# A fused Nyström-attention and Fourier-MLP kernel: Pool takes a share of VectorE's work at the start, and the inverse's iterations carry B instead of C·v

## The chip, the cores and the metric

The kernel runs on one core of one Trainium2 chip. The metric is the device time of one execution in microseconds (us). The engines that matter are TensorE (PE in the profile, with PEld for its weight loads), VectorE (DVE), ScalarE (ACT), GpSimd (POOL) and SyncE (SP), which issues all DMAs. The kernel before takes 1015.25 us, the median of three runs (1013.77 to 1017.46).

## The reference

Eight batches, eight heads, 576 tokens, head size 64. The first half is attention by 32 landmarks, with an iterated inverse; the second half is a real 2-D Fourier transform, a layer norm and an MLP from 512 to 2048 and back. The weights come as float64, the rest as float32.

```python
def sm(a, b):                        # softmax of scale * a @ b.T
    ...
q_lm, k_lm = means of q and k over 18 tokens (32 landmarks)
A, Bm, C = sm(q, k_lm), sm(q_lm, k_lm), sm(q_lm, k)
Z = Bm.T / (norm1(Bm) * norminf(Bm) + 1e-6)
for _ in range(6):
    Z = 2 * Z - Z @ Bm @ Z
x = A @ Z @ C @ v                    # heads joined: (8, 576, 512)
u = x + real(fft(fft(x, axis=1), axis=2))
un = (u - mean(u)) / sqrt(var(u) + 1e-6)
out = u + relu(un @ w_ch1) @ w_ch2
```

## The kernel before, in words

**Two halves on one TensorE.** Every float32 matrix that needs its precision is split into a high and a low float16 half (`split`, line 245: ACT writes the high half, DVE the rest by one SCALAR_TENSOR_TENSOR) and multiplied in three float16 matmuls (`mm3`). The MLP is the bulk: tokens go in chunks of 256 (`TCH` = 2 tiles of 128), and each chunk multiplies with sixteen pieces of w1 (output `h` in PSUM, 256 columns) and sixteen pieces of w2 (accumulators `acc`, 512 columns). `mlp` (line 879) runs the chunks, with the w2 products two steps behind the w1 products.

**Attention, per batch.** `tokens` (line 410) takes the landmark sums, the scales, splits q (two halves `e` of the heads, line 459), makes the softmax A (three blocks `u`, lines 468 to 495), A's transposed halves, and A's folds over mirrored tokens (F1, F2, Fh, lines 518 to 528), whose product with cosine and sine tables is `CS`. `landmarks` (line 552) makes the softmaxes B and C, sets up the inverse (E and RE, lines 637 to 643), transposes C's exponentials, multiplies them by v (lines 669 to 679), runs six iterations on the pair RE (lines 683 to 696), and then forms the landmark weights Wx and Wt and their table product WC. RE has 96 columns for each of two groups of heads: 32 hold the power of the residual matrix, 64 hold C·v, which the iterations multiply by the inverse as they go. A block-diagonal B (`Bbd`) comes in at the end. `mix` (line 743) puts A, WC, Wx and CS together into the rows `u`, and `norm` (line 816) normalises them and hands them to the MLP as `unT`, the transposed halves. For the first two batches transposes go over TensorE, later ones over DMA transposes.

**Weights.** `weights` (line 265) decodes each float64 piece of 128x512 as it lands: ACT makes its magnitude (`prepare`, four pieces ahead, `PREP`), a low part comes from DVE (even pieces: a shift, line 332) or ACT (odd pieces: a byte conversion, line 335), and DVE joins the two (line 336). Pieces feed a Gram matrix on TensorE (`squares`), from which a scale comes (`scale`, after 18 decoded pieces for w1, after all 32 for w2). `halve` (line 312) then splits a piece by that scale.

**What sets the order.** The order of TensorE's work is written out by a planner: the generators above are threads with priorities (attention, weights, MLP, line 948 on), `now` is a model of TensorE's time, `Timed` (line 114) models the other engines by a fixed and a per-element cost, and `till` (line 224) makes a thread wait until its inputs should be ready, and, with `banks`, until that many PSUM banks should be free. While a thread waits, others put matmuls into the queue; while all wait and the accumulator bank is not yet in use, filler matmuls on `idle` are issued. TensorE then executes that order as it stands, waiting wherever the model was too early. The instructions of the other engines are ordered by the framework, and `Timed` adds order constraints that keep VectorE and ScalarE from waiting for late inputs.

Of the kernel before, what the change touches and what calls it, by code (L numbers as in the profile page):

```python
# [18 lines left out]
P = 128  # L19
# [94 lines left out]
class Timed:  # L114
# [6 lines left out]
    def __getattr__(self, name):  # L121
        call = getattr(self.engine, name)

        def emit(out, *args, **kw):
# [5 lines left out]
            start = max([self.kernel.now] + [self.kernel.there.get(a.name, 0.0) for a in aps])  # L130
            end = max(self.free, start + self.fixed + rate * n + 0.1)
            self.kernel.there[out.name] = end
            for a in aps[1:]:
                self.kernel.read[a.name] = end
# [4 lines left out]
            late = max([late] + [self.kernel.there.get(a.name, 0.0) for a in aps if a.name in self.kernel.slow and a is not out])  # L139
            if self.engine is self.kernel.nc.gpsimd:  # L140
                self.kernel.slow.add(out.name)
            else:
                self.kernel.slow.discard(out.name)
# [10 lines left out]
class Kernel:  # L154
    def __init__(self, ctx, tc, NB, q, k, v, w1, w2, t1, t1t, t2, diag, mask, out):
# [7 lines left out]
        self.loads = {}  # L163
# [12 lines left out]
        self.whole = [self.cp.tile([P, 512 * NF + OFF], F32, name=f"w{w}") for w in range(2)]  # L176
        self.mask = const(mask, [P, 6], F32, "mask")
# [26 lines left out]
        self.arrival(1.7)  # L204

# [59 lines left out]
    def weights(self):  # L265
# [12 lines left out]
        def prepare(i):  # L278
# [6 lines left out]
            mags.append(mag)  # L285

# [9 lines left out]
        def scale(w):  # L296
# [4 lines left out]
            yield self.till(a2)  # L301
# [10 lines left out]
        def halve():  # L312
            w, f = pieces[sum(self.split_w)]
            self.split(hl[w][f][:, 0], hl[w][f][:, 1], slots[w][f], sc[:, w : w + 1])
            self.split_w[w] = f + 1

        for i, (w, f) in enumerate(pieces):
# [10 lines left out]
            low = self.wraw[i].rearrange("p (m x) -> p m x", x=2)[:, :, 0]  # L328
            x, dst = mags[i].bitcast(I32), slots[w][f].bitcast(I32)
            (A if i % 2 else V).late = self.raw_there[i]  # L330
            if i % 2 == 0:
                V.tensor_scalar(dst, low, 29, None, ALU.logical_shift_right)
            else:
                byte = self.wraw[i].bitcast(mybir.dt.uint8).rearrange("p (m x) -> p m x", x=8)[:, :, 3]
                A.activation(dst, byte, AF.Copy, scale=2.0**-5, bias=-0.484375)
# [6 lines left out]
            yield max(0.0, max(self.V.free, self.G.free) - self.now - WT)  # L342
            if i == NF + 1:
                yield from scale(0)
            for _ in range(PACE if es else 0):
                if self.split_w[0] < NF:
                    halve()
                    yield max(0.0, max(self.V.free, self.G.free) - self.now - WT)
# [61 lines left out]
    def tokens(self, b, st):  # L410
# [33 lines left out]
        yield self.till(kb, more=AM) + (HOLD if b == 1 else 0.0)  # L444
# [14 lines left out]
        for e in range(2):  # L459
            qs = loads[e][1][:, 0:NQ].rearrange("p (x t) -> p x t", t=2 * SEG)  # L460
            for t, a, w in ((qm[e], 1, 128), (qr[e], 129, 16)):
                split(*(t[:, y].rearrange("p r (s t) -> p (r s) t", t=w) for y in range(2)), qs[:, :, a : a + w], rq)
# [5 lines left out]
        for u in range(3):  # L468
            yield self.till(*qhs)
# [24 lines left out]
            (self.G if b > 0 else V).tensor_tensor(av, av, bc(asum), ALU.mult)  # L494
# [24 lines left out]
        for x, op in enumerate((ALU.add, ALU.subtract)):  # L519
            V.tensor_tensor(F1[x], aes[0], aes[1], op)  # L520
        for x, op in enumerate((ALU.add, ALU.subtract)):
            F2 = self.mid()[:, 0:512]
            for k in range(2):
                (V if x == 0 else G).tensor_tensor(F2[:, 256 * k : 256 * k + 256], F1[k][:, 0:256], F1[k][:, 256:512], op)
# [4 lines left out]
        Fs.append(hl)  # L529
        CS = self.big().bitcast(F16).rearrange("p (g y x t) -> p g y x t", g=2, y=2, x=2)  # L530
# [20 lines left out]

    def landmarks(self, b, st):
# [7 lines left out]
        RE = sm.tile([P, 2, 96], F32, name="RE", bufs=3)  # L560
# [60 lines left out]
        yield self.till(nrm)  # L621
# [12 lines left out]
        Bbd = sm.tile([P, 2, 4, 32], F32, name="Bbd", bufs=1)  # L634
        V.tensor_tensor(Bbd, wide(nrm[:, :, 0, :], 32), m4g(32), ALU.mult)
        yield self.till(BTd, Ces[0])
# [7 lines left out]
        ETs = []  # L644
        for g in range(2):
            if b < 2:
# [405 lines left out]
```

## Time and profile before

| | |
|---|---|
| median of three runs | 1015.25 us |
| the profiled execution | 1017.3 us |
| its span, first to last instruction | 1015.5 us |
| busy: PE, DVE, ACT, POOL | 961.4, 595.1, 332.1, 125.8 us |
| filler matmuls on `idle` | 22.0 us |

In the profile L137 is the line of the helper through which DVE, ACT and POOL instructions go, and L233 that of the matmul helper, so groups are told apart by the names of the tiles. The tile `w` holds both weights, `at` is a working PSUM bank, `big`, `mid` and `row` are working buffers. A busy share of PE counts the filler too. In a timeline each row has its start, its length (several like instructions in a row merged, with their count), the engine, and in brackets how long the engine sat idle before it and what ended that.

### The profile page before, as it was taken

The page shows a single profiled execution, that of the slowest core. Times are in us where ns is not written, and L with a number is a line of the kernel's source. Part 1 is how long each engine was busy: PE and PEld are TensorE (multiplying, and loading weights), DVE is VectorE, ACT ScalarE, POOL GpSimd, SP SyncE. Part 2 cuts the span into 40 slices and gives each one's busy share as a digit, 9 for nine tenths or more (in the row PEclk, how much of TensorE's full clock was granted, in tenths as well). Part 3 has the DMA queues.
Part 4 walks back from the last instruction along what each step waited for, and adds up shares of the span by engine and source line. Part 5 has one row for each costly group of instructions (what it writes and reads, how often), then busy time and mean ns, then how long its engine had stood idle before and what let it go on. Part 6 is the DMA issues. An engine that isn't in the chain of part 4 may idle for free.

```text
span 1015.5 us, 20853 instructions
## 1 busy us (share of the span) xinstructions
PE 961.4 (95%) x8701; PEld 667.2 (66%) x8701; DVE 595.1 (59%) x1599; ACT 332.1 (33%) x708; POOL 125.8 (12%) x144
## 2 busy tenths in 40 slices
PE   6769889899999999999999999999999999999998
PEld 4658556567665777666666677666666676666665
DVE  7889776886367636386267736784463834351111
ACT  5668643243134213153134213332322322111110
POOL 0000000014011400123001400231020310110000
PEclk8979999899999999999999999999999999999999
DMA  9854104133302430134202240225020200120000
GB/s 329 284 207 154 53 1 167 22 66 83 122 6 62 93 121 2 42 58 108 84 24 41 51 167 1 63 48 180 1 54 21 49 13 22 21 53 21 1 21 21
DMA packets 97774, 74.66 MB, mean 74 GB/s; under 512 B 68112, under 2 KB 86544, under 8 KB 97552
## 3 DMA queue, kind: packets, MB, share of 16 engines
q1 hardware_dynamic: 97680, 73.34, 24.7%
q8 instruction: 68, 1.11, 0.5%
q14 instruction: 26, 0.21, 0.1%
HBM read 48.02 MB, written 9.44 MB: 57 GB/s over the span
## 4 chain that ended last, share of the span: by engine, by line
PE 45%; issue 23%; DVE 6%; POOL 3%; DMA 2%; ACT 1%; SPq 0%; POOLq 0%; DVEq 0%; ACTq 0%
PE h L233 20%; PE acc L233 20%; PE at L233 6%; POOL mid L137 1%; DVE mid L137 1%; POOL row L137 1%; DMA mid<-mid 1%; DVE big L137 1%; DVE h L137 1%; DVE asum L137 1%; DVE row L137 1%; DVE u L137 1%; DMA unT<-row 0%; SPq L661 0%; DMA out_dram<-u 0%
## 5 line engine op out<-in xcount | busy, mean ns | idle before, releaser
L233 PE MATMUL h<-unT,w 128*128 128x256 f16 x3456 | 411.9, 273 | 3.9 <-DMA unT<-row 2.5
L233 PEld LDWEIGHTS <-w 128*128 128x128 f16 (+1 forms) x3584 | 345.7, 98 | 77.9 <-issue 7.9
L233 PE MATMUL acc<-w,h 128*128 128x512 f16 x1632 | 386.1, 382 | 2.4 <-DVE w L137 2.4
L233 PEld LDWEIGHTS <-h 128*128 128x128 f16 x1632 | 157.9, 99 | 167.8 <-issue 14.5
L137 DVE SCALAR_TENSOR_TENSOR h<-h 128x512 f16<-128x512 f32 x136 | 93.4, 687 | 196.6 <-ACT h L137 196.1
L137 ACT ACTIVATE h<-h 128x512 f16<-128x512 f32 x136 | 80.9, 595 | 300.8 <-PE h L233 288.4
L137 POOL TENSOR_TENSOR r<-ve,mhalf 128x2 f32<-128x2 f32 (+1 forms) x20 | 13.7, 684 | 475.9 <-DVE ve L137 471.3
L137 POOL TENSOR_TENSOR mid<-mid 128x640 f16<-128x640 f32 (+2 forms) x36 | 40.4, 1144 | 99.7 <-ACT mid L137 82.7
L137 DVE TENSOR_TENSOR mid<-mid 128x256 f32<-128x256 f32 (+3 forms) x52 | 39.6, 796 | 12.5 <-POOL mid L137 6.4
L137 DVE TENSOR_REDUCE lm<-big 128x32 f32<-128x576 f32 (+1 forms) x48 | 44.2, 939 | 3.3 <-DMA big<-k_dram 3.1
L233 PEld LDWEIGHTS <-big 128*128 128x128 f16 (+1 forms) x864 | 40.2, 103 | 8.2 <-issue 2.1
L137 DVE SCALAR_TENSOR_TENSOR u<-at,scw,row 128x128 f32<-128x128 f32 (+3 forms) x120 | 38.7, 389 | 9.7 <-DMA out_dram<-u 6.9
L137 ACT CAST row<-row 128x512 f16<-128x512 f32 (+1 forms) x40 | 20.7, 551 | 72.0 <-DVE row L137 72.0
L233 PEld LDWEIGHTS <-mid 64*128 64x128 f16 (+1 forms) x624 | 30.2, 96 | 20.4 <-issue 13.9
L137 POOL TENSOR_TENSOR row<-row 128x512 f16<-128x512 f32 (+1 forms) x33 | 35.5, 1091 | 32.9 <-ACT row L137 32.9
L137 DVE SCALAR_TENSOR_TENSOR row<-at,scw,row 128x262 f32<-128x262 f32 (+1 forms) x48 | 21.4, 486 | 29.9 <-ACT row L137 20.2
L233 PE MATMUL at<-RE,E 128*128 128x96 f32 (+1 forms) x192 | 30.8, 279 | 8.6 <-DVE RE L137 8.6
L233 PEld LDWEIGHTS at<-RE,E 128*128 128x128 f32 x192 | 27.1, 192 | 16.1 <-DVE RE L137 9.4
L137 DVE SCALAR_TENSOR_TENSOR u<-acc,wsc,u 128x512 f32<-128x512 f32 x36 | 26.7, 748 | 11.1 <-PE acc L233 10.9
L137 DVE TENSOR_TENSOR E<-at,mask 128x256 f32<-128x256 f32 x40 | 16.6, 416 | 28.0 <-PE at L233 28.0
L233 PE MATMUL at<-mid,big 128*128 128x262 f16 (+1 forms) x288 | 32.7, 282 | 0.1
L137 DVE SCALAR_TENSOR_TENSOR big<-big,aq_r 128x1024 f16<-128x1024 f32 (+1 forms) x32 | 25.8, 840 | 3.5 <-ACT big L137 3.5
(174 smaller groups left out, 911.0 us busy)
## 6 DMA issues: line engine op xcount, KB each, us to landing
w<-w_dram SPq DMA_DIRECT2D x22, 512.0 KB, 7.0
big<-v_dram SPq DMA_DIRECT2D x16, 640.0 KB, 9.4
big<-q_dram SPq DMA_DIRECT2D x16, 584.0 KB, 5.6
big<-k_dram SPq DMA_DIRECT2D x16, 576.0 KB, 4.6
out_dram<-u SPq DMA_DIRECT2D x36, 256.0 KB, 2.0
big<-w_dram SPq DMA_DIRECT2D x10, 512.0 KB, 4.7
t<-t_dram SPq DMA_DIRECT2D x1, 1048.0 KB, 10.3
unT<-row SPq DMA_TRANSPOSE x64, 2.4
```

Of the source, the lines that this page charges most:

```text
L137: ins = call(out, *args, **kw)
L233: self.nc.tensor.matmul(out, a, b, start=start, stop=stop, skip_group_check=True)
```

## The change

Pool (`self.G`) takes these from VectorE: the low part of the even weight pieces, now a byte conversion, issued in `prepare`; the two elementwise steps of every third piece's halving (high half still by ScalarE); for batches 0 and 1 the scaling and low half of q for e = 1, the differences of F2 and the low half of the second Fh; for batch 0 the scaling of A's softmax and the difference of F1.

The inverse's iterations carry B (32 columns) in place of C·v (64 columns); the result is made block-diagonal (`Yd`) and multiplied by `R0`, the scaled C·v, at the end. C's transposes and its product with v move into a thread of their own, `values`, which runs beside the iterations. Pool's instructions are held in the order in which the program issues them. Seven waits of the planner now also count a free PSUM bank (`banks=1`), the weights' pace no longer counts Pool's time, times are kept per offset for tiles that are one allocation, and for batches after 0 two buffers of `mix` lie in memory that the raw weights no longer need.

```diff
@@ Timed.emit
-            start = max([self.kernel.now] + [self.kernel.there.get(a.name, 0.0) for a in aps])
+            key = self.kernel.key
+            start = max([self.kernel.now] + [self.kernel.there.get(key(a), 0.0) for a in aps])
...
             if self.engine is self.kernel.nc.gpsimd:
-                self.kernel.slow.add(out.name)
+                self.kernel.slow.add(key(out))
+                if self.log:
+                    info = mybir.DependencyInfo(mybir.DependencyClass.NoSync, mybir.DependencyReason.DATA)
+                    self.kernel.tc.add_manual_dep(ins.ins, self.log[-1][1], info, reason="order")
+                self.log.append((start, ins.ins.name))
@@ weights, prepare
+            E = (self.G, A)[i % 2]
+            byte = self.wraw[i].bitcast(mybir.dt.uint8).rearrange("p (m x) -> p m x", x=8)[:, :, 3]
+            if i % 2 == 0:
+                E.tensor_scalar(dst, byte, 2.0**-5, -0.484375, ALU.mult, ALU.add)
+            else:
+                E.activation(dst, byte, AF.Copy, scale=2.0**-5, bias=-0.484375)
@@ weights, halve
-            self.split(hl[w][f][:, 0], hl[w][f][:, 1], slots[w][f], sc[:, w : w + 1])
+            if f % 3 == 2:
+                self.G.tensor_scalar(slots[w][f], slots[w][f], sc[:, w : w + 1], None, ALU.mult)
+                A.copy(hl[w][f][:, 0], slots[w][f])
+                self.G.tensor_tensor(hl[w][f][:, 1], slots[w][f], hl[w][f][:, 0], ALU.subtract)
+            else:
+                self.split(hl[w][f][:, 0], hl[w][f][:, 1], slots[w][f], sc[:, w : w + 1])
@@ weights, the loop over pieces
-            if i % 2 == 0:
-                V.tensor_scalar(dst, low, 29, None, ALU.logical_shift_right)
-            else:
-                ...
-            yield max(0.0, max(self.V.free, self.G.free) - self.now - WT)
+            yield max(0.0, self.V.free - self.now - WT)
@@ tokens
-        yield self.till(kb, more=AM) + (HOLD if b == 1 else 0.0)
+        yield self.till(kb, banks=1, more=AM) + (HOLD if b == 1 else 0.0)
...
+            if b < 2 and e == 1:
+                self.G.tensor_scalar(loads[e][1][:, 0:NQ], loads[e][1][:, 0:NQ], rq, None, ALU.mult)
...
+                if b < 2 and e == 1:
+                    A.copy(hi, qs[:, :, a : a + w])
+                    self.G.tensor_tensor(lo, qs[:, :, a : a + w], hi, ALU.subtract)
...
-            (self.G if b > 0 else V).tensor_tensor(av, av, bc(asum), ALU.mult)
+            self.G.tensor_tensor(av, av, bc(asum), ALU.mult)
...
-            V.tensor_tensor(F1[x], aes[0], aes[1], op)
+            (V if b > 0 or x == 0 else self.G).tensor_tensor(F1[x], aes[0], aes[1], op)
...
-                (V if x == 0 else G).tensor_tensor(F2[...], F1[k][:, 0:256], F1[k][:, 256:512], op)
+                (V if x == 0 else self.G).tensor_tensor(F2[...], F1[k][:, 0:256], F1[k][:, 256:512], op)
...
-            G.tensor_tensor(Fh[:, 1], F2, Fh[:, 0], ALU.subtract)
+            (V if b < 2 and x == 0 else self.G).tensor_tensor(Fh[:, 1], F2, Fh[:, 0], ALU.subtract)
@@ landmarks (C's transposes and its product with v move unchanged into values(), which writes R0)
-        RE = sm.tile([P, 2, 96], F32, name="RE", bufs=3)
+        RE = sm.tile([P, 2, 64], F32, name="RE", bufs=3)
...
-        Bbd = sm.tile([P, 2, 4, 32], F32, name="Bbd", bufs=1)
-        V.tensor_tensor(Bbd, wide(nrm[:, :, 0, :], 32), m4g(32), ALU.mult)
+        A.copy(RE[:, :, 32:64], nrm[:, :, 0, :])
+        self.spawn(self.values(b, st, loads, Ces, crs, ci))
...
-                mm(ps[:, 96 * g + c0 : 96 * g + 96], E[:, g].rearrange("p a b -> p (a b)"), RE[:, g, c0:])
+                mm(ps[:, 64 * g + c0 : 64 * g + 64], E[:, g].rearrange("p a b -> p (a b)"), RE[:, g, c0:])
...
-            yield self.till(E, RE, more=NM)
+            if it < 5:
+                yield self.till(E, RE, banks=1, more=NM)
+        Yd = sm.tile([P, 2, 4, 32], F32, name="Yd", bufs=1)
+        V.tensor_tensor(Yd, wide(RE[:, :, 32:64], 32), m4g(32), ALU.mult)
+        while "R0" not in st:
+            yield 0.3
+        R0 = st["R0"]
+        yield self.till(Yd, R0, banks=2, more=NM)
...
-            mm(ps[:, 64 * g : 64 * g + 64], Bbd[:, g].rearrange("p a b -> p (a b)"), RE[:, g, 32:])
+            mm(ps[:, 64 * g : 64 * g + 64], Yd[:, g].rearrange("p a b -> p (a b)"), R0[:, g])
...
         yield self.till(Wt, banks=2)
+        while b < 2 and not st.get("folds"):
+            yield 0.3
```

More of the change, by code (lines that the diff above doesn't have):

```diff
@@ L129, in emit @@
             self.free = max(self.free, self.kernel.now) + self.fixed + rate * n
-            start = max([self.kernel.now] + [self.kernel.there.get(a.name, 0.0) for a in aps])
+            key = self.kernel.key
+            start = max([self.kernel.now] + [self.kernel.there.get(key(a), 0.0) for a in aps])
             end = max(self.free, start + self.fixed + rate * n + 0.1)
-            self.kernel.there[out.name] = end
+            self.kernel.there[key(out)] = end
             for a in aps[1:]:
-                self.kernel.read[a.name] = end
+                self.kernel.read[key(a)] = end
             if "accum_out" in kw:
@@ L138, in emit @@
             late, self.late = self.late, 0.0
-            late = max([late] + [self.kernel.there.get(a.name, 0.0) for a in aps if a.name in self.kernel.slow and a is not out])
+            late = max([late] + [self.kernel.there.get(key(a), 0.0) for a in aps if key(a) in self.kernel.slow and a is not out])
             if self.engine is self.kernel.nc.gpsimd:
-                self.kernel.slow.add(out.name)
+                self.kernel.slow.add(key(out))
[3 more added lines that the diff above has]
+                self.log.append((start, ins.ins.name))
             else:
-                self.kernel.slow.discard(out.name)
+                self.kernel.slow.discard(key(out))
                 prev = next((p for s, p in reversed(self.log) if s <= late), None)
@@ L162, in __init__ @@
         self.ps_at, self.ps_h, self.ps_o = psum("ps_at", 8 - PSH - TCH), psum("ps_h", PSH), psum("ps_o", 1)
-        self.loads = {}
+        self.loads, self.places = {}, set()
         self.now, self.there, self.read, self.used = 0.0, {}, {}, []
@@ L176, in __init__ @@
         self.whole = [self.cp.tile([P, 512 * NF + OFF], F32, name=f"w{w}") for w in range(2)]
+        self.places = {t.name for t in self.whole}
         self.mask = const(mask, [P, 6], F32, "mask")
@@ L204, in __init__, with key @@
         self.arrival(1.7)
+    def key(self, a):
+        if a.name not in self.places:
+            return a.name
+        return a.name, a.offset
     def psum(self):
@@ L285, in prepare @@
             mags.append(mag)
+            w, f = pieces[i]
+            dst = slots[w][f].bitcast(I32)
+            E = (self.G, A)[i % 2]
+            E.late = self.raw_there[i]
+            byte = self.wraw[i].bitcast(mybir.dt.uint8).rearrange("p (m x) -> p m x", x=8)[:, :, 3]
[3 more added lines that the diff above has]
+                E.activation(dst, byte, AF.Copy, scale=2.0**-5, bias=-0.484375)
         def squares(i):
@@ L300, in scale @@
             V.tensor_reduce(a2, dg, AX.X, ALU.add)
-            yield self.till(a2)
+            yield self.till(a2, banks=1)
             ps = self.psum()
@@ L468, in tokens @@
         for u in range(3):
-            yield self.till(*qhs)
+            yield self.till(*qhs, banks=1)
             ps = self.psum()
@@ L620, in landmarks @@
             crs.append(cr)
-        yield self.till(nrm)
+        yield self.till(nrm, banks=1)
         psn = self.psum()
@@ L761, in mix @@
                 self.folded = b
-            Qs = self.row(NC)
-            Tt = self.row(528).rearrange("p (x m) -> p x m", x=2)
+            if b == 0:
+                Qs, Tt = self.row(NC), self.row(528)
+            else:
+                Qs, Tt = self.whole[0][:, 512 * NF : 512 * NF + NC], self.whole[1][:, 512 * NF : 512 * NF + 528]
+            Tt = Tt.rearrange("p (x m) -> p x m", x=2)
             A.activation(Qs[rows], pss[other, 0:NC], AF.Copy, scale=x2[other])
```

99 lines of the change are left out of this document (51 added, 48 removed).

## The prediction

> **What bounds the kernel now.** I read the page first (engines, slices), then busy time by stage, then TensorE's own waits and timeline, then VectorE and Pool by shape.
>
> ```profile
> span 1015.5 us, 20853 instructions
> ...
> PE 961.4 (95%) x8701; PEld 667.2 (66%) x8701; DVE 595.1 (59%) x1599; ACT 332.1 (33%) x708; POOL 125.8 (12%) x144
> ...
> PE   6769889899999999999999999999999999999998
> ...
> DVE  7889776886367636386267736784463834351111
> ...
> POOL 0000000014011400123001400231020310110000
> ```
>
> Each digit of a slice is a tenth of 25 us. TensorE is full from slice 11 on; VectorE is full only at the left, where Pool is empty. The stages, cut where the timeline changes (PE, PEld, DVE, ACT, POOL busy, then clock and DMA):
>
> ```profile
> 0.00:74.50 74.50, 50.09 (x576) 38.92 (x577) 62.53 (x189) 44.46 (x95) 3.33 (x10) 0.86 0.81 278
> 74.50:113.00 38.50, 36.35 (x387) 31.95 (x385) 33.79 (x74) 28.36 (x53) 1.62 (x2) 1.00 0.42 138
> 113.00:150.00 37.00, 30.18 (x330) 16.85 (x329) 30.59 (x85) 20.48 (x40) 0.00 (x0) 0.95 0.01 2
> 150.00:260.00 110.00, 103.72 (x960) 70.70 (x958) 79.86 (x221) 38.79 (x87) 17.68 (x22) 0.97 0.35 99
> 260.00:1015.50 755.50, 741.03 (x6458) 508.76 (x6455) 388.36 (x1034) 199.98 (x435) 103.21 (x110) 1.00 0.19 50
> ...
> L233 PE MATMUL acc<-idle,ones 128*128 128x256 bf16 x131 | 22.0, 308 | 2.4 <-ACT ones L186 2.4
> ```
>
> The last row is from TensorE by group: 22.0 us of the busy time is filler, nearly all of it before the MLP starts. So the end is set by three things: when the MLP's first matmul comes, TensorE's work after it, and the gaps. After 260 us TensorE idles 755.5 - 741.0 = 14.5 us in all. The points that matter in its timeline:
>
> ```profile
> 74.55 0.82 PE L233 MATMUL h<-unT,w 128*128 128x256 f16 x6
> ...
> 127.54 2.54 PE L233 MATMUL acc<-w,h 128*128 128x512 f16 x11 [2.43 <-DVE w L137]
> ...
> 135.59 0.16 PE L233 MATMUL at<-kb,ones 128*128 128x1 bf16 x1 [4.32 <-ACT mid L137]
> 135.61 5.08 PE L233 MATMUL acc<-w,h 128*128 128x512 f16 x15
> ...
> 365.56 2.75 PE L233 MATMUL acc<-w,h 128*128 128x512 f16 x12
> ...
> 469.00 0.46 PE L233 MATMUL at<-RE,E 128*128 128x96 f32 x2 [1.50 <-DVE RE L137]
> ...
> PE at L233 <- DVE RE L137: 4.2, 5, 1.5
> ```
>
> The first MLP matmul is at 74.55 us; VectorE is busy 62.53 us of the 74.5 before it. Whatever shortens VectorE's queue there moves everything behind it. The matmul on `kb` waits 4.32 us for a PSUM bank that ACT's exponentials still read. Behind it fifteen matmuls take 5.08 us, where later twelve take 2.75: at the later pace fifteen take 3.4, so 1.6 us more are lost to a lower clock (0.95 in that stage). The last row, from TensorE's waits after 260 us, says that iterations waited 4.2 us for RE, five times.
>
> **The change: the inverse.** Fewer columns save little:
>
> ```profile
> 363.18 0.58 PE L233 MATMUL at<-RE,E 128*128 128x96 f32 x4
> 363.60 2.13 PE L233 MATMUL h<-unT,w 128*128 128x256 f16 x18
> ...
> 373.13 0.55 PE L233 MATMUL at<-RE,E 128*128 128x64 f32 x4
> 373.52 0.81 PE L233 MATMUL acc<-w,h 128*128 128x512 f16 x3
> ```
>
> From a group's start to the next group's, four matmuls hold TensorE for 0.42 us at 96 columns and 0.39 at 64. So 8 batches x 5 iterations x 0.03 = **-1.2 us**; the sixth (64 to 32) is taken as nothing. Yd replaces Bbd and R0 replaces RE's 64 columns in the final products, at equal shapes: nothing. The one ACT copy of B into RE is hidden, as ACT is at a third of its time.
>
> The waits for RE come in the middle of an iteration's four matmuls (two go, two wait, as at 469.00): the second group's C·v is late. With C·v in its own thread this wait goes; next late is the following power of E, which the planner spaces by margins. Of 4.2 us I take **-3.5**. The DMA transposes of C that move with it (SP queue, batches 2 on) pass no load, since the next batch's loads are issued at `mix`; they have six iterations as cover, as R0 is needed only after the last (363 to 373 us shows 5 us for each iteration). Without that cover their wait would be what 469.00 shows, 1.5 us a batch.
>
> **The bank waits.** With `banks=1` the planner lets the MLP's matmuls go first, and the halves they need are mostly there (VectorE was halving w2 then). 4.3 + 1.6 = 5.9 us are at stake, nothing at the least; I take **-5**.
>
> **Pool's share.** VectorE by shape, start to 250 us, and the unhindered 128x512 difference in its timeline:
>
> ```profile
> L137 DVE SCALAR_TENSOR_TENSOR w<-w,wsc 128x512 f16<-128x512 f32 x32 | 23.8, 745 | 1.7 <-ACT w L137 1.2
> L137 DVE SCALAR_TENSOR_TENSOR w<-row,w 128x512 int32<-128x512 int32 x32 | 21.8, 684 | 0.9 <-ACT w L137 0.6 <-ACT row L137 0.2
> ...
> L137 DVE SCALAR_TENSOR_TENSOR big<-big,aq_r 128x1024 f16<-128x1024 f32 x6 | 7.7, 1277 | 0.0
> ...
> L137 DVE TENSOR_TENSOR mid<-mid 128x256 f32<-128x256 f32 x10 | 5.0, 536 | 0.0
> ...
> L137 DVE TENSOR_SCALAR w<-w 128x512 int32<-128x512 int32 x11 | 4.5, 418 | 0.0
> ...
> L137 DVE TENSOR_TENSOR mid<-mid 128x512 f16<-128x512 f32 x4 | 2.7, 686 | 0.0
> ...
> L137 DVE SCALAR_TENSOR_TENSOR big<-big,aq_r 128x128 f16<-128x128 f32 x6 | 2.1, 343 | 0.0
> ...
> L137 DVE TENSOR_TENSOR mid<-mid,asum 128x512 f32<-128x512 f32 x2 | 1.4, 680 | 0.0
> ...
> 34.56 0.69 DVE L137 TENSOR_TENSOR mid<-mid 128x512 f32<-128x512 f32 x1
> ```
>
> VectorE is relieved, before the first h: 9 shifts (the scale of w1 comes after 18 pieces) x 0.418 = 3.8; q for e = 1, 1.28 + 0.34 = 1.6; the softmax, 2 x 0.68 = 1.4; F1 0.7; F2 2 x 0.54 = 1.1; Fh 0.7. Sum 9.3. From there to 113 us: 7 shifts 2.9, 5 of 16 halvings x 0.745 = 3.7; sum 6.6. After 113: 5 halvings 3.7, batch 1's q, F2, Fh 3.4; sum 7.1. In all 23.0 us.
>
> Pool's price (after 250 us; the memset from the start):
>
> ```profile
> L137 POOL TENSOR_TENSOR row<-row 128x512 f16<-128x512 f32 x27 | 31.0, 1166 | 32.9 <-ACT row L137 32.9
> ...
> L137 POOL TENSOR_TENSOR mid<-mid,asum 128x512 f32<-128x512 f32 x10 | 10.5, 1046 | 46.1 <-DVE asum L137 46.1
> L137 POOL TENSOR_TENSOR mid<-mid 128x256 f32<-128x256 f32 x10 | 8.7, 890 | 1.3 <-DVE mid L137 1.3
> ...
> L200 POOL MEMSET Wx<- 128x1024 f16 x1 | 1.0, 955 | 0.0
> ```
>
> The trace has no byte conversion and no scaling by one operand on Pool. From below the memset bounds it, 0.48 us for 512; from above the 1.17 of a two-operand difference; I take 1.05, the float32 product of the same size. Before the first h: 9 bytes 9.5, q's scaling of 1168 columns 2.4 and its differences of 1152 2.6, softmax 2.1, F1 1.05, F2 1.8, Fh 1.2; sum 20.6. Then to 113 us 7 x 1.05 + 5 x 2.22 = 18.4, after that about 19. In all 58 us, where Pool idles today, so it fits. But the two engines collide:
>
> ```profile
> 344.90 1.19 POOL L137 TENSOR_TENSOR row<-mid,row 128x512 f16<-128x512 f32 x1 [0.37 <-ACT row L137]
> ...
> 345.26 1.38 DVE L137 TENSOR_TENSOR mid<-mid 128x512 f32<-128x512 f32 x1
> ...
> 348.85 2.27 POOL L137 TENSOR_TENSOR mid<-mid 128x512 f16<-128x512 f32 x2 [0.20 <-ACT mid L137]
> ...
> 349.31 0.69 DVE L137 SCALAR_TENSOR_TENSOR h<-h 128x512 f16<-128x512 f32 x1 [0.91 <-ACT h L137]
> ...
> 130.30 0.72 ACT L137 ACTIVATE w<-w,wsc 128x512 f16<-128x512 f32 x1 [1.21 <-DVE w L137]
> ```
>
> VectorE's op of 0.69 us took 1.38 beside Pool's 1.19: it stood until Pool was through. So 0.69 of 1.19, 58% of Pool's time, came back as VectorE's wait. An op on `h`, which lies in PSUM, kept its 0.69 beside Pool's 2.27. (The last row, ACT's half of a weight split, is for a rival.) Before the first h about a third of VectorE's busy time is in ops with both operands in SBUF like this one (18 joinings x 0.684 = 12.3, the other half of q, folds). By that share 19% of Pool's time is lost, if every two-operand op is always met 58%; I take 30%, nearer to the lower end because ops that read PSUM, like that on `h`, go by. The Trainium skill's page "SBUF — State Buffer", section "Who interferes with whom", says that a VectorE instruction with two SBUF inputs and a Pool instruction that reads SBUF take the shared port as an exclusive lock. By that rule, the trace agrees: 1.38 against 0.69.
>
> At 30%: first h 9.3 - 6.2 = **-3.1 us** (both what it needs, unT and the first halves, end in VectorE); then 6.6 - 5.5 and 7.1 - 5.7 leave 2.5, of which only TensorE's wait for `w` at 127.54, 2.43 us, can take anything: **-1.5**.
>
> **What is added.** Pool in program order waits first in, first out: a byte conversion whose weights have not landed holds q's scaling, the softmax and the norm's small power behind it, and TensorE waits for those through `unT`. The wait for R0 and the wait for the folds are the planner's alone. A new order finds new gaps: after 260 us the 14.5 us of idle are 4.2 for RE and some 10 others; I charge a third of those, **+3.1**.
>
> Sum: -1.2 - 3.5 - 5 - 3.1 - 1.5 + 3.1 = **-11.2 us**. The profiled execution took 1017.3 (span 1015.5), 2.05 over the median, so 1006.1 there and 1004 for the median of 1015.25. With Pool's loss at 19% to 40%, the bank at -2 to -5.9 and the added gaps at 0 to +6, this case has its own range of 998 to 1010.
>
> **Rivals.** *The lock eats more than the relief (slower).* At 58% of 58 us VectorE waits 34 us for a relief of 23: first h +2.6, w2's halves +4.1, batch 1 +3.9. Then the halves are late, so the bank's place can't be filled: 10.6 - 3.5 - 1.2 + 3.1 = +9, 1024 us. It turns the sign from about 50% on, where 58 x 0.5 - 23 = 6 meets the other gains. For it: VectorE is full before 75 us, and small ops with two operands are met too. Against it: the ops on PSUM.
>
> *The relief arrives whole.* Pool's one-operand ops cost near the memset and fall beside PSUM ops: at 10%, first h -7.2, `w` -2.4, bank -5.9, RE -4.2, columns -1.2, added +1: -20, 995 us. For it: Pool starts bytes pieces ahead of need.
>
> *Given back in the halves.* Every third piece goes Pool, ACT, Pool: 1.05 + 0.72 + 1.17 = 2.9 us, against 0.72 + 0.745 = 1.5 now, and TensorE takes pieces in order. Ten pieces late by 1.4 are 14 us; with some in hand, about 10: -1, 1014 us, no change. Against it: two of three pieces still come from VectorE, so Pool has a lead.
>
> **Numbers.** Forecast 0.53, lock 0.17, whole relief 0.15, given back 0.15. Under 0.3% (3 us) a measurement of this kernel cannot tell a change from none. So faster 0.68, same 0.15, slower 0.17. The range 996 to 1019 leaves out most of the lock's case and the lower part of the whole relief's.
>
> **What would show it.** Right: the first h at about 71 us; no 4 us wait before the matmul on `kb`; no wait for RE in mid-iteration; groups of 64 columns at 0.39 us; w<-row,w at over 0.75 us mean before 113 us (0.684 now), which is the lock. Wrong: the first h at 75 or later with joinings of 0.9 us and more (lock); waits for `w` after Pool in TensorE's list (given back); the first h near 67 (whole relief); a byte conversion on Pool of 1.5 us or more would make the Pool sum, and with it the forecast, too small.

## The result, and the profile after

The changed kernel takes 1030.24 us, median of four runs (1027.82 to 1031.20), against 1015.08 for the kernel before on the same chip: ratio 1.0149, 95% interval 1.0126 to 1.0172. It is 15 us slower where the prediction had it 11 us faster, and outside the range of 996 to 1019. The profiled execution took 1027.8 us (span 1025.6).

From the page of the kernel after: span, busy times, and the slices of 25.6 us for TensorE, VectorE and Pool.

```profile
span 1025.6 us, 20864 instructions
...
PE 966.5 (94%) x8675; PEld 668.8 (65%) x8675; DVE 595.9 (58%) x1559; ACT 334.4 (33%) x716; POOL 193.2 (19%) x196
...
PE   5768869999999999999999999999999999999998
...
DVE  7777786698465846278366836683552845151111
...
POOL 3325451101302130013111311122020120010000
```

Pool took 67 us of work (125.8 to 193.2), and VectorE gave up nothing: 595.1 before, 595.9 now. Busy time in the stages, cut at the same events as before: the first MLP matmul, the first w2 matmul, and 260 us (PE, PEld, DVE, ACT, POOL, then clock and DMA):

```profile
0.00:84.40 84.40, 55.68 (x555) 41.55 (x556) 65.28 (x171) 44.95 (x95) 28.30 (x32) 0.76 0.71 246
84.40:129.00 44.60, 38.29 (x359) 31.37 (x358) 31.85 (x62) 28.93 (x54) 22.08 (x17) 0.88 0.38 120
...
260.00:1025.60 765.60, 755.81 (x6597) 520.26 (x6595) 394.00 (x1045) 206.63 (x450) 109.21 (x117) 1.00 0.20 54
```

The first stage is 9.9 us longer (84.4 against 74.5) and the second 6.1 us (44.6 against 38.5). In both VectorE has more idle time than before, not less: 84.4 - 65.3 = 19.1 us against 74.5 - 62.5 = 12.0, and 12.7 against 4.7. The granted clock is 0.76 and 0.88 in these stages, against 0.86 and 1.00; no run holds it fixed, so whether it adds to the loss or only follows from TensorE's idle time is not shown. After 260 us TensorE idles 765.6 - 755.8 = 9.8 us where it idled 14.5, so the steady part gained about what the prediction said. All of the loss, and more, lies in the start. The two waits that the prediction watched, in TensorE's timeline:

```profile
84.39 0.79 PE L245 MATMUL h<-unT,w 128*128 128x256 f16 x5
...
155.34 0.16 PE L245 MATMUL at<-kb,ones 128*128 128x1 bf16 x1 [7.92 <-ACT mid L138]
```

The first `h` comes at 84.4 us, and the bank wait at `kb` has grown from 4.32 to 7.92 us.

The lock is the prediction's word for VectorE standing until an instruction on Pool is through. VectorE's timeline shows it on instructions that take 0.2 to 0.35 us by themselves, and Pool's timeline shows what they stood behind:

```profile
14.23 1.97 DVE L138 TENSOR_TENSOR Bd<-Bd,bmx 128x64 f32<-128x64 f32 x1
...
23.31 2.16 DVE L138 SCALAR_TENSOR_TENSOR klm<-lm,sc,klm 128x128 f16<-128x128 f32 x1
```

```profile
12.63 3.75 POOL L138 TENSOR_SCALAR big<-big,aq_r 128x1168 f32<-128x1168 f32 x1
...
23.08 2.68 POOL L138 TENSOR_TENSOR big<-big 128x1024 f16<-128x1024 f32 x2 [6.70 <-ACT big L138]
...
95.40 1.21 POOL L138 TENSOR_SCALAR w<-w 128x512 int32<-128x512 uint8 x1
96.69 2.07 POOL L138 TENSOR_SCALAR w<-w,wsc 128x512 f32<-128x512 f32 x1
99.50 1.16 POOL L138 TENSOR_TENSOR w<-w 128x512 f16<-128x512 f32 x1 [0.73 <-ACT w L138]
100.74 0.65 POOL L138 TENSOR_SCALAR w<-w 128x512 int32<-128x512 uint8 x1
101.49 2.41 POOL L138 TENSOR_SCALAR w<-w,wsc 128x512 f32<-128x512 f32 x1
```

`Bd` and `klm` end within 0.3 us of Pool's instruction (16.2 and 25.5 against 16.4 and 25.8). The group that the prediction named, the joinings, over the first 165 us (mean 789 ns, where it was 684):

```profile
L138 DVE SCALAR_TENSOR_TENSOR w<-row,w 128x512 int32<-128x512 int32 x32 | 25.1, 789 | 6.6 <-ACT w L138 3.5 <-POOL w L138 2.5 <-ACT row L138 0.5
```

Summed over all shapes (count times mean, against the lowest mean of that shape in the kernel before or in a run without reads on Pool), VectorE's instructions in the first 165 us are 17.3 us longer than they need be, beside 68.2 us of Pool's time: 25%. The same sum gives 0.5 us for the kernel before and 1.5 to 1.8 for runs in which Pool only writes, so it is good to some 2 us. The last five of Pool's rows show something else: from 91.9 to 112 us Pool goes round a weight's scaling, ACT's half, Pool's difference and a byte conversion, with hardly a gap but its waits for ACT's half (0.73 us each). The chain of waits between 80 and 135 us goes through it. Its summary, and its pieces from 91 to 104 us (start, length, what):

```profile
by line: POOL w L138 22.6%; PE h L245 18.9%; ACT w L138 10.5%; issue 8.2%; PE at L245 7.7%; ACT row L138 7.4%; DVE w L138 4.8%; PE acc L245 4.4%; PE at L250 3.5%; ACT big L138 3.4%; DVE u L138 1.8%; ACT u L138 1.8%; POOL r L138 1.3%; DVE un
...
91.86 1.57 POOL w L138
93.45 0.63 ACT w L138
94.15 1.15 POOL w L138
95.40 1.21 POOL w L138
96.69 1.95 POOL w L138
98.64 0.81 issue
99.50 1.16 POOL w L138
100.74 0.65 POOL w L138
101.49 2.42 POOL w L138
103.93 1.19 ACT w L138 x2
```

Pool, the engine that was to be a helper with time to spare, is the first name in the chain of this stage.

### The profile page after: what moved, and what is told of

Its sections match the earlier page's. It is cut to its first block, busy times and chain, and to the rows that moved or that the text cites. A ratio compares the mean times of both kernels' runs of the same rounds, so it can differ in the third digit from the quotient of the medians.

```text
span 1025.6 us, 20864 instructions
## 1 busy us (share of the span) xinstructions
PE 966.5 (94%) x8675; PEld 668.8 (65%) x8675; DVE 595.9 (58%) x1559; ACT 334.4 (33%) x716; POOL 193.2 (19%) x196
## 4 chain that ended last, share of the span: by engine, by line
PE 80%; DVE 8%; ACT 3%; POOL 3%; issue 2%; DMA 2%; SPq 1%; DVEq 0%; POOLq 0%; ACTq 0%
PE acc L245 34%; PE h L245 33%; PE at L245 13%; POOL w L138 2%; DVE w L138 1%; DVE u L138 1%; DVE lm L138 1%; POOL mid L138 1%; DVE mid L138 1%; ACT w L138 1%; DMA big<-k_dram 1%; ACT row L138 1%; PE at L250 1%; ACT mid L138 1%; DVE h L138 1%
## 5 line engine op out<-in xcount | busy, mean ns | idle before, releaser
L138 POOL TENSOR_TENSOR r<-ve,mhalf 128x2 f32<-128x2 f32 (+1 forms) x20 | 13.3, 666 | 400.0 <-DVE ve L138 388.6
L138 POOL TENSOR_TENSOR mid<-mid 128x256 f32<-128x256 f32 (+3 forms) x43 | 45.6, 1080 | 128.2 <-ACT mid L138 107.9
L138 DVE TENSOR_REDUCE lm<-big 128x32 f32<-128x576 f32 (+1 forms) x48 | 44.6, 942 | 3.2 <-DMA big<-k_dram 2.5
L245 PEld LDWEIGHTS <-mid 64*128 64x128 f16 (+1 forms) x624 | 30.8, 98 | 20.0 <-issue 13.3
L138 DVE TENSOR_TENSOR mid<-mid 128x256 f32<-128x256 f32 (+3 forms) x45 | 38.7, 876 | 7.2 <-DMA mid<-mid 4.5
L138 DVE SCALAR_TENSOR_TENSOR u<-at,scw,w 128x128 f32<-128x128 f32 (+3 forms) x105 | 33.9, 391 | 5.9 <-PE at L245 4.2
L138 POOL TENSOR_TENSOR mid<-mid,asum 128x512 f32<-128x512 f32 x16 | 16.7, 1047 | 95.1 <-DVE amx L138 60.3
L138 DVE SCALAR_TENSOR_TENSOR w<-at,scw,w 128x262 f32<-128x262 f32 (+1 forms) x42 | 19.2, 487 | 25.9 <-ACT w L138 25.8
L138 DVE SCALAR_TENSOR_TENSOR u<-acc,wsc,u 128x512 f32<-128x512 f32 x36 | 26.7, 747 | 12.2 <-PE acc L245 12.2
L245 PE MATMUL at<-RE,E 128*128 128x64 f32 (+1 forms) x192 | 28.8, 273 | 5.1 <-DVE RE L138 4.2
L138 DVE SCALAR_TENSOR_TENSOR w<-row,w 128x512 int32<-128x512 int32 x32 | 25.1, 789 | 6.6 <-ACT w L138 3.5
## 6 DMA issues: line engine op xcount, KB each, us to landing
t<-t_dram SPq DMA_DIRECT2D x1, 1048.0 KB, 10.5
```

The costliest lines, as they stand in the source:

```text
L138: ins = call(out, *args, **kw)
L245: self.nc.tensor.matmul(out, a, b, start=start, stop=stop, skip_group_check=True)
```

## The experiments

Three questions: which part of the change costs, by what mechanism, and what each part is worth by itself. In all runs below the ratio is to the kernel before on the same chip.

### Pool's shares, taken back

`no_pool_share` gives all four shares back to VectorE and keeps the rest (inverse, values thread, waits). `q_back`, `halves_back` and `bytes_back` each give one back.

```diff
 no_pool_share: all of these, and the softmax and folds as before
 q_back:      - if b < 2 and e == 1:          + if False:
 halves_back: - if f % 3 == 2:                + if False:
 bytes_back:  - E.tensor_scalar(dst, byte, 2.0**-5, -0.484375, ALU.mult, ALU.add)
              + V.tensor_scalar(dst, low, 29, None, ALU.logical_shift_right)
```

The edits are shortened here: `low` stands for the low words of the raw piece, and the shift stands ahead of the joining, as in the kernel before.

> All four shares that Pool took go back to VectorE (even bytes as a shift, every third halving, q's e = 1, the softmax and folds of batches 0 and 1); the inverse with B, the thread for C times v, the bank waits and Pool's program order stay. If Pool's share is the cause, the first h comes back to 72 to 76 us (84.4 in the changed kernel, 74.55 before) and, as the changed kernel idles 9.8 us after 260 us against 14.5, the time is 1007 to 1013. If the new order of the planner or the inverse is the cause, it stays at 1025 to 1031.

Measured: 1016.09, ratio 1.0023 (1.0011 to 1.0035).

> Only q's e = 1 goes back to ACT and VectorE, in batches 0 and 1. Theory A (the chain of batch 0: q's scaling of 3.75 us and its differences of 2.7 on Pool hold the small ops of the inverse's set-up and the softmax of A, which starts at 33.9 us against 25.8): first h at about 76 to 78 us and 1020 to 1023. Theory B (the lock takes a share of all of Pool's time, whichever op it is): q is 11 of some 68 us on Pool, its relief 3.2 us, so 1028 to 1031. Theory C (a byte or a halving late in Pool's order): 1028 to 1031.

Measured: 1027.52, ratio 1.0136 (1.0116 to 1.0156).

> Only the halvings of every third piece go back to ACT and VectorE. Theory A: the first h stays at 83 to 85 us, 1026 to 1031. Theory B: 29 of 68 us of Pool's time go, with them some 7 us of the lock, and 7.4 us of relief: 1028 to 1032. Theory C: TensorE's waits for w after Pool and ACT (1.6, 0.85 and 0.45 us) and VectorE's waits for Pool's w (7.3 us, ten times) go: 1021 to 1026.

Measured: 1022.03, ratio 1.0075 (1.0059 to 1.0091).

> Only the low parts of the even weight pieces go back to VectorE as shifts at the join. Theory A: 1027 to 1033. Theory B: 15.6 of 68 us of Pool's time go, about 4 us of the lock, against 6.7 us of relief: 1030 to 1034. Theory C (bytes behind the softmax in Pool's order hold up the joinings: one runs at 28.8 us, the next at 42.4): the joinings of the first 20 pieces come earlier, the first h at 78 to 80, 1022 to 1026.

Measured: 1016.91, ratio 1.0030 (1.0018 to 1.0042).

Pool's share costs 1.0149 - 1.0023, 12.8 us. The bytes alone bring 12 of them back and the halves alone 7.5, so the parts do not add. The scaling of q, which was the first suspect because A's softmax came 8 us late (33.9 us against 25.8), is worth 1.3 us, which is not clear of noise: with q on VectorE the softmax came at 26.7 us, but the scale of w1, which waits for the decoding, then came at 81.6 us against 76.4. Without any share the kernel is still 2.3 us slower than before.

### Pairs of shares

> Bytes and q both go back; Pool keeps the halvings and the softmax and folds of batches 0 and 1. Theory D, formed from the first runs: the first h waits for the later of two chains, attention of batch 0 (delayed by q on Pool) and the decoding of w1 (delayed by the bytes on Pool), so that q alone gave only 1.4 us and bytes alone 12. Then both together bring the first h to 75 to 77 us and the time to 1011 to 1015. If the effects merely saturate (no share at all gives 1016), 1015 to 1018.

Measured: 1019.45, ratio 1.0048 (1.0029 to 1.0067).

> Bytes and halvings back with VectorE; Pool keeps q, the softmax and the folds of batches 0 and 1. Separately they gave 12 and 7 us. If the losses of the two lie one behind the other (bytes before the first h, halvings after it), they add up to 1009 to 1012; if the first only makes room that the second fills, 1014 to 1018.

Measured: 1015.48, ratio 1.0018 (1.0006 to 1.0030).

> Only the softmax of batch 0 and the folds of batches 0 and 1 go back; Pool keeps bytes, halvings and q. Their time on Pool is 14 of some 68 us, the relief 7 us. If the loss goes by Pool's time, 1026 to 1029; if bytes are late because they stand behind these in Pool's order, 1018 to 1023.

Measured: 1025.33, ratio 1.0120 (1.0089 to 1.0150); here the softmax and the folds of batches 0 and 1 alone are back on VectorE. That is 2.9 us less than with all shares on Pool, not clear of noise either.

The idea that two chains (weights and attention) run side by side and the later one decides, so that bytes and q together must bring all back, fell: that pair is not better than the bytes alone. Bytes and halves together are: with q, softmax and folds still on Pool the time is that of no share at all, although VectorE's instructions are still 9.8 us longer in that run. By stages:

| | first h | first w2 matmul | between |
|---|---|---|---|
| before | 74.6 | 113.2 | 38.7 |
| after | 84.4 | 129.0 | 44.6 |
| halves back | 84.5 | 120.6 | 36.1 |
| bytes back | 79.4 | 119.5 | 40.1 |
| bytes and halves back | 78.9 | 117.2 | 38.3 |

The byte conversions cost 5 us before the first `h` and 4.5 us behind it, the halves 8.5 us behind it and nothing ahead. With the bytes gone the halves cost little (40.1 against 38.3; 1.0030 against 1.0018). Then no byte conversion stands between two halvings in Pool's queue, which is the likely reason; no run tests it by itself. TensorE's waits in `bytes_back`, between its first h and its first w2 matmul, name the rest:

```profile
PE h L245 <- POOL w L138: 2.0, 2, 1.1
PE h L245 <- ACT w L138: 1.8, 1, 1.8
```

### Pool's order

```diff
-                if self.log:
+                if False:
                     info = mybir.DependencyInfo(mybir.DependencyClass.NoSync, mybir.DependencyReason.DATA)
```

> The changed kernel without the constraint that keeps Pool in program order. If bytes and halvings wait behind the softmax because of that order (theory C), the framework puts them ahead: first h at 78 to 80 us, time 1018 to 1024. If the order that results is the same, 1027 to 1031.

Measured: 1034.76, ratio 1.0197 (1.0174 to 1.0221). The program's order on Pool does not cause the loss; without it the kernel is some 5 us slower still, and the first `h` comes at 88.6 us.

### The lock by itself

To the kernel before, instructions on Pool are added at the start that nobody waits for: 30 products of 128x384 (`dummy_read`, shown here), or 60 memsets of the same tile (`dummy_write`), and later 18 products (`reads18`).

```diff
+        self.junk = self.cp.tile([P, 384], F32, name="junk")
+        nc.gpsimd.memset(self.junk, 0.0)
+        for _ in range(30):
+            nc.gpsimd.tensor_tensor(self.junk, self.junk, self.junk, ALU.mult)
```

> The kernel before, with 30 extra Pool multiplications of a 128x384 buffer by itself at the start, whose result nobody uses (about 24 us of Pool time from 3 us on, reading SBUF). No relief, no other order. If the lock by itself costs what a share of Pool's time suggests (23% in the changed kernel's trace, summed over the lengthened VectorE ops), batch 0's chain and the first h come 4 to 7 us later and the time rises by 4 to 7 us. If the lock is hidden by slack, 0 to 2 us.

Measured: 1022.30, ratio 1.0074 (1.0050 to 1.0097).

> The kernel before, with 60 extra Pool memsets of the same buffer at the start (about the same Pool time, but nothing read). If what costs is the shared reading of SBUF, this is at the kernel before within 2 us, and VectorE's ops with two operands keep their 0.69 us. If any Pool work at all disturbs VectorE, it costs as much as the reading one.

Measured: 1014.33, ratio 1.0007 (0.9992 to 1.0021).

> The kernel before with 18 products of 128x384 on Pool from the start whose result nobody uses (30 of them cost 7.5 us). Theory lock at full price: 18/30 of it, 4.5 us, ratio 1.0035 to 1.0055. Rival (only those late in the run, on the way to A, counted): 1.000 to 1.002.

Measured: 1018.51, ratio 1.0039 (1.0026 to 1.0053).

In Pool's groups of the first 165 us the two loads are of one size (busy time, mean ns, idle before); the first row is `dummy_read`'s, the second `dummy_write`'s.

```profile
L209 POOL TENSOR_TENSOR junk<-junk 128x384 f32<-128x384 f32 x30 | 28.2, 938 | 2.4
```

```profile
L209 POOL MEMSET junk<- 128x384 f32 x60 | 25.4, 424 | 3.5
```

Thirty instructions that read lengthen VectorE's by 8.8 us and the kernel by 7.5; eighteen, 15.7 us of Pool's time, lengthen them by 3.4 and the kernel by 4.0 (2.6 to 5.4). Sixty that only write do nothing that can be measured. In the kernel before, the lock thus costs close to its full length. The Trainium skill's page "SBUF — State Buffer", section "Who interferes with whom", says that a VectorE instruction with two SBUF inputs contends with a Pool instruction that reads SBUF and not with one that only writes it. These runs agree: 7.5 us against nothing.

### The relief by itself

`relief_only` is the kernel before with VectorE's moved instructions left out and, for most of them, memsets on Pool in their place, which `dummy_write` shows to cost nothing; `relief_reads18` is the same with the eighteen products of `reads18`.

```diff
-            if i % 2 == 0:
-                V.tensor_scalar(dst, low, 29, None, ALU.logical_shift_right)
...
+            if f % 3 == 2:
+                A.activation(hl[w][f][:, 0], slots[w][f], AF.Copy, scale=sc[:, w : w + 1])
+                nc.gpsimd.memset(hl[w][f][:, 1], 0.0)
```

> The kernel before, from which VectorE's share that the change gives to Pool is left out, and Pool gets only memsets of the outputs in its place: the low three bits of the even weight pieces, the low halves of every third weight piece and of q for e = 1 in batches 0 and 1, the division of A's softmax in batch 0, and the differences in F1, F2 and the second Fh. So the relief of 23 us without Pool's reading and without its latency. If the relief is worth what the prediction's sum took for it (9.3 us before the first h, all of it on the path), the first h comes at 64 to 67 us and the time is 1002 to 1007. Rival theory E (VectorE in order spends what is freed on waits, as in the changed kernel, where it idles 19.1 us before the first h against 12.0): first h at 70 to 73, time 1009 to 1012.

Measured: 1012.49, ratio 0.9996 (0.9979 to 1.0013).

> The kernel before with VectorE's moved work left out and Pool writing constants in its place (so the low parts of even weight pieces, the low halves of every third weight piece and of half of q in batches 0 and 1, a division of A's softmax and some folds are not computed), and with the same 18 products on Pool from the start. Theory (relief lies beside the path, the lock on it, so they do not cancel): 4 to 5 us over the relief alone, ratio 1.003 to 1.006. Rival, the prediction's sum (relief of 23 us pays for 5 us of lock): 0.998 to 1.001, as the relief alone.

Measured: 1013.99, ratio 1.0001 (0.9988 to 1.0015).

Taking the work off VectorE gains nothing that can be measured, although the first `h` comes 3.3 us earlier (71.25 us) and batch 1's first product of `t` and `mid` 9 us earlier (157.0 against 166.3). The stages of `relief_only` show where it goes:

```profile
0.00:74.50 74.50, 51.34 (x601) 38.89 (x602) 60.89 (x178) 47.41 (x100) 6.97 (x19) 0.86 0.82 281
...
260.00:1010.30 750.30, 733.88 (x6413) 504.92 (x6411) 386.22 (x1028) 198.95 (x432) 103.22 (x110) 1.00 0.19 50
```

TensorE has 51.3 us of work there instead of 50.1, and the lead is used up later; after 260 us TensorE idles 750.3 - 733.9 = 16.4 us against 14.5, with 6.5 us of waits for RE. The planner's model counts the work that is left out, so TensorE's order is another one in this run: it shows what the relief is worth with the order that comes of it. The second run contradicts what I expected of it. The eighteen products that cost 4.0 us in `reads18` cost 0.5 us on top of the relief, which is within noise (VectorE's instructions are 4.2 us longer in it, against 1.8 in `relief_only`). So relief does pay for the lock. It is a cushion: VectorE can be later by about as much as it was relieved, and being earlier bought nothing in these runs.

### The inverse and the waits

`no_share_no_banks` is `no_pool_share` with nine bank waits out as well: the seven new ones, and two that the kernel before has too, for A's exponentials (`ae`) and for the MLP's `unT`. So it doesn't take the waits back to what they were, as its expectation says. `values_inline` is `no_pool_share` with C's transposes and product for batches 0 and 1 in their old place; `inline_share` the same with all of Pool's shares.

```diff
-        self.spawn(self.values(b, st, loads, Ces, crs, ci))
+        if b < 2:
+            yield from self.values(b, st, loads, Ces, crs, ci)
+        else:
+            self.spawn(self.values(b, st, loads, Ces, crs, ci))
```

> The inverse with B and the thread for C times v alone: Pool's share goes back and the waits for free banks go back to what they were. Beside the run without Pool's share (1016): if the bank waits gain what was predicted (5 us), this is at 1019 to 1022; if they cost, by moving matmuls back in the order at the start, it is at 1010 to 1014; if they do nothing, 1015 to 1017.

Measured: 1015.95, ratio 1.0033 (1.0016 to 1.0050). The nine together do nothing that can be measured; the seven by themselves were not run.

> The kernel after with Pool's four shares back on VectorE, and for batches 0 and 1 C's transposes and its product with v where they were, before the iterations, not in a thread of their own. Theory order (the thread runs ahead of the weights in the plan, so the sum for w1's scale is put behind the first block's transposes and mix, 75.46 us against 66.92, and the first h waits for halves): wsc at 70 us or earlier against 76.8, first h at 74 to 75 against 77.7, and the steady gain after 260 us stays (idle near 10 us against 14.5): 1009 to 1012, ratio 0.995 to 0.998. Rival (the loss is the iterations' own: B's copy by ACT, the shorter groups, the planner's seven waits): first h and time as without Pool's share, 1.001 to 1.004.

Measured: 1020.67, ratio 1.0064 (1.0047 to 1.0082).

> The kernel after with all of Pool's shares, and for batches 0 and 1 C's transposes and product with v where they were. Theory (lock and late Pool results are the most of the loss, the order of the thread 3 us of it): 1024 to 1029, ratio 1.009 to 1.013. Rival (the thread's order is what Pool's shares collide with): below 1.006.

Measured: 1032.28, ratio 1.0178 (1.0161 to 1.0196). Both of the last two are slower than with the thread, and the first `h` comes later in both: at 79.3 us against 77.7, and at 93.0 against 84.4. Neither was expected.

My explanation for the 2.3 us was one point in the plan: the sum for w1's scale (`wm`) goes into TensorE's queue behind the first block's transposes, where before it went ahead of them. The two orders in TensorE's timeline, `no_pool_share` and then the kernel before:

```profile
71.03 1.94 PE L250 MATMUL at<-ident,row 128*128 128x128 f32 x8 [1.97 <-DVE row L138]
...
74.97 0.28 PE L245 MATMUL at<-wm,ones 128*128 128x1 f32 x2
...
77.74 0.39 PE L245 MATMUL h<-unT,w 128*128 128x256 f16 x2 [0.84 <-ACT w L138]
```

```profile
66.92 0.56 PE L233 MATMUL at<-wm,ones 128*128 128x1 f32 x2 [3.97 <-DVE wm L137]
...
69.26 1.94 PE L238 MATMUL at<-ident,row 128*128 128x128 f32 x8 [1.54 <-DVE row L137]
```

With the values inline the sum does go first, and the kernel is slower still. Its TensorE and VectorE:

```profile
74.94 1.94 PE L250 MATMUL at<-ident,row 128*128 128x128 f32 x8 [8.89 <-DVE row L138]
```

```profile
65.64 0.13 DVE L138 TENSOR_SCALAR wsc<-wp_r 128x1 f32<-128x1 f32 x1
...
66.60 0.74 DVE L138 SCALAR_TENSOR_TENSOR w<-w,wsc 128x512 f16<-128x512 f32 x1
...
72.44 0.75 DVE L138 SCALAR_TENSOR_TENSOR w<-w,wsc 128x512 f16<-128x512 f32 x1
...
73.59 0.74 DVE L138 SCALAR_TENSOR_TENSOR w<-w,wsc 128x512 f16<-128x512 f32 x1
74.26 1.00 DVE L138 TENSOR_SCALAR row<-u,mv,r 128x512 f32<-128x512 f32 x2
```

Now the scale is ready at 65.6 us, the halvings that it sets free stand between the steps of the norm on VectorE, and TensorE waits 8.9 us for the normalised rows. The kernel before lies between: norm at 68.6 us, scale at 69.6. My explanation by the scale alone fell; the two runs suggest that either order of the two chains on VectorE can be the wrong one, but the thread changes more of the plan than this order.

So the last run leaves the start alone: the kernel before, with the new iterations and the values thread (with its one bank wait) for batches 2 to 7 only.

```diff
+        if b < 2:
             V.tensor_tensor(Bbd, wide(nrm[:, :, 0, :], 32), m4g(32), ALU.mult)
             yield self.till(BTd, Ces[0])
+        else:
+            A.copy(RE[:, :, 32:64], nrm[:, :, 0, :])
+            self.spawn(self.values(b, st, loads, Ces, crs, ci))
+            yield self.till(BTd)
...
-            c0 = 0 if it < 5 else 32
+            c0, W = 0 if it < 5 else 32, 96 if b < 2 else 64
```

> The kernel before, with the new inverse and the values thread for batches 2 to 7 alone; batches 0 and 1, the weights, Pool and the bank waits as before, so the plan of the start is before's to the instruction. Theory (the inverse's steady gain is real, its loss is all in a reshuffled start): first h at 74.5 us, idle of TensorE after 260 us near 10 us against 14.5, 1007 to 1011 us, ratio 0.994 to 0.998. Rival (the steady gain is only idle moved from one place to another, or the longer way through R0 gives it back): 0.999 to 1.002.

Measured: 1006.68 (1006.33 to 1008.40), ratio 0.9939 (0.9925 to 0.9952). By the ratios it beats the kernel before by 6.2 us and the kernel after by some 21. Its stages, and TensorE's largest wait after 260 us:

```profile
0.00:74.50 74.50, 51.52 (x598) 40.17 (x600) 63.45 (x191) 45.49 (x97) 3.32 (x10) 0.89 0.82 278
...
260.00:1004.50 744.50, 733.98 (x6434) 505.04 (x6431) 389.14 (x1028) 200.82 (x438) 104.21 (x110) 1.00 0.19 50
```

```profile
PE at L233 <- DVE RE L137: 2.4, 2, 2.0
```

The first `h` comes at 73.3 us, 1.2 earlier than in the profile before, although the start's order of matmuls is the same: the granted clock was 0.89 there against 0.86, and the run does not say why. After 260 us TensorE idles 10.5 us instead of 14.5, and waits 2.4 us for RE instead of 4.2.

## Why the prediction was wrong, point by point

**The step that failed** is Pool's share: "At 30%: first h 9.3 - 6.2 = -3.1 us", with the sentence before it that 58 us are "where Pool idles today, so it fits". Its sum was -4.6 us (first h and the wait for `w`), and the share measured +12.8. Three things in it:

- *The lock's share was right.* 30% forecast, 25% measured in the kernel after, 31% beside the thirty dummy reads (8.8 of their 28.2 us), 22% beside the eighteen. Pool's total was right too: 68.2 us in the first 165, less the 7.6 of the kernel before, is 60.6 against 58. Single prices were off: a scaling of 512 columns takes 1.57 us undisturbed and 1.75 in the mean where 1.05 was taken, q's scaling 3.5 where 2.4 was taken. A byte conversion takes 0.65 us undisturbed, but 0.97 in the mean of the 16, because VectorE holds Pool as well (see the last section); so the 1.05 taken was near for a reason that the sum did not have.
- *The relief was counted at face value.* It gains nothing by itself (0.9996): 9.3 us taken off VectorE before the first `h` bring it 3.3 us forward, and the end not at all. So whatever VectorE's busy share of 84% there seemed to say, VectorE's amount of work was not what the end waited for. As a cushion it works: a lock that costs 4.0 us without it costs nothing measurable under it. This makes the subtraction 9.3 - 6.2 right in its sign and worth zero, not -3.1.
- *Pool's own time was left out of the path.* A moved step takes longer on Pool and stands in one queue with the others: scaling, ACT, difference and a byte conversion in a row, with 22.6% of the chain from 80 to 135 us. Giving the halves back saves 7.5 us, nearly all behind the first `h`; giving the bytes back saves 12, half of it ahead.

How much of the 13.3 us that bytes and halves cost together is lock, and how much is Pool's late results, the runs don't separate. The lengthening falls by 7.5 us when both are taken back (17.3 to 9.8), so at a full microsecond each at least 5.8 us are not VectorE's lengthening. The 9.8 us that stay cost nothing, which fits the cushion.

**The bank waits**, -5 predicted: nothing came that the runs can measure. In the kernel after the wait at `kb` is 7.92 us; without Pool's share it is 2.76 us with the bank waits and 3.71 without the nine, and the times differ by less than noise (1.0023 and 1.0033). The planner counts a bank as free by its own model of the reads, which has no lock; that this is why the wait stayed is argued, not shown. The 4.3 + 1.6 us at stake were also read from one execution. `late_inverse` has the same order there, and its rows are

```profile
134.62 0.16 PE L233 MATMUL at<-kb,ones 128*128 128x1 bf16 x1 [2.63 <-ACT mid L137]
134.64 3.40 PE L233 MATMUL acc<-w,h 128*128 128x512 f16 x15
```

with 2.63 us of wait and nothing lost to a lower clock behind it.

**The inverse**, -1.2 and -3.5: right in sign and about right in size. With the start left alone it gives -6.2 us (0.61%, 4.9 to 7.6) for six of eight batches. The columns were right: a group of 64 holds TensorE for 0.39 us. Of the waits for RE the run took 1.8 us, not 3.5; the idle time after 260 us fell by 4.0 in all, so other waits gave more than was forecast. About 1.2 us of the 6.2 are the earlier first `h`, which the inverse does not explain.

**The added gaps**, +3.1: this is the term that was most undersized after Pool's. Without Pool's share the kernel is 2.3 us slower than before, and the inverse is worth -6.2, so by difference the other edits and the new order of batches 0 and 1 cost about 8.5 us, if the parts add. I charged a third of the steady gaps for it; the loss is in the start, where two chains meet on VectorE. Which of the edits there does it (thread, wait for the folds, earlier conversions by ACT, the weights' new pace, new iterations in the first two batches) is open; taking the thread alone back made it worse.

Together: -6.2 + 8.5 + 12.8 = 15.1 us, against 15.2 measured; as the 8.5 is a difference, this closes by construction and proves nothing.

**The rivals.** "The lock eats more than the relief" gave 1024, the nearest, and its sign was right, but its mechanism asked for a lock share over 50%, and it was 25%. "Given back in the halves" named the row of Pool, ACT, Pool and 10 us; the halves measured 7.5 with the bytes in the same queue, and without them 1.2, which is not clear of noise. It was one of two such rows; the prediction did not see that the byte conversions stand in the other. "The relief arrives whole" gave 995, and fell with `relief_only`: with no lock at all the relief gains nothing.

## What to carry to other kernels

An engine that is busy for 84% of a stage need not be what the stage waits for: leave some of its work out once, before counting relief as gain. A helper engine with idle time still has a queue and a longer duration for each step, so a moved step is priced by its own chain (wait, duration, what stands ahead of it) and not only by the sum of its time. And in a start where several chains meet, try a steady gain with the start untouched: the inverse gave +0.2% together with the other edits of the start (Pool's share left out) and -0.6% with the start left alone.

## What the runs showed of the hardware

Instructions with one operand in SBUF are held by Pool too. `bs`, 128x2, takes 0.15 us, and stood until Pool's scaling was through:

```profile
151.47 2.26 DVE L138 TENSOR_SCALAR bs<-bs 128x2 f32<-128x2 f32 x1
```

```profile
150.47 3.24 POOL L138 TENSOR_SCALAR big<-big,aq_r 128x1168 f32<-128x1168 f32 x1
```

The Trainium skill's page "SBUF — State Buffer", section "Who interferes with whom", says that `tensor_scalar` can enter a mode that takes both ports and then contends, so this is not outside its rule. The prediction had counted two-operand instructions alone.

VectorE holds Pool too. The byte conversion at 95.40 us, shown above, took 1.21 us, where the one at 100.74 took 0.65; it began beside this halving and ended about 0.5 us after it:

```profile
95.34 0.75 DVE L138 SCALAR_TENSOR_TENSOR w<-w,wsc 128x512 f16<-128x512 f32 x1 [1.20 <-POOL w L138]
```

The 16 conversions of the start are some 5 us longer by this than 16 at 0.65, and the ten scalings 1.8 us longer than at 1.57.

On Pool a scaling by one operand is not cheaper than an instruction with two: 1.57 us for 512 float32 columns against 1.05 for a product of the same size and 1.16 for a difference. The Trainium skill's page "GPSIMD Engine Reference", section "Engine selection", calls one-input work there roughly line-rate. For this scaling by one number per partition the trace does not agree: on VectorE the TENSOR_SCALAR that writes a 128x512 float32 `row` takes 0.54 us in the kernel before. Pool's byte conversion by constants comes nearer, with 0.65 us for 512.
